# GFNet mixing with a SiLU MLP: another layout for one spill in DRAM, and another order for the conversion of the weights in the first twelve steps

## The chip, the core and the metric

The kernel runs on one core of a Trainium2 chip. The core has a matrix engine (TensorE, "PE" in the profile, with its weight loads listed apart as "PEld"), a vector engine (VectorE, "DVE"), a scalar engine (ScalarE, "ACT"), GpSimd ("POOL") and SyncE ("SP", which here only issues DMAs). Every engine works through its own queue in order, and waits where an instruction needs a result of another engine or of a DMA. The metric is the time of one execution on the device in microseconds (us).

## The reference

Eight sequences of 3008 rows with 256 channels each go through a filter in the frequency domain, and the result through a two-layer network with SiLU:

```python
X = np.fft.rfft(x, axis=1)
F = (filt_r + 1j * filt_i)[None, :, :]
y = np.fft.irfft(X * F, n=x.shape[1], axis=1)       # 8 x 3008 x 256
x = y.reshape(8 * 3008, 256)
h = x @ w_in                                        # 256 x 2048
out = (h * (1.0 / (1.0 + np.exp(-h)))) @ w_out      # 2048 x 256
```

The weights of the network arrive in 64-bit floats, the rest is used in 32-bit.

## The kernel before, in words

**Two halves.** The filter ("spectral part" of a batch entry `b`, the function `spectral`) is a DFT in stages with intermediate results in two DRAM tiles, `d1` and `d2`. The network takes tokens in pairs of blocks (`pairs`: 48 blocks of 2 x 256 or 2 x 240 tokens), and for each pair goes through the 2048 hidden channels in 8 steps of 256 (`jp` = 0 to 7). There are 384 steps. In step `s` TensorE alternates between a product of `hidden(s)` (the first layer) and one of `project(s - 1)` (the second layer), in 8 rounds. Pieces of the next batch entry's spectral part are put into these rounds: `put(step, round, piece, ...)` adds a piece to a list, and the loop at the end of the kernel emits, after every round, the pieces that are due. The order of every engine's queue is thus written out by hand; no scheduler moves anything.

**The opening.** Before step 0 stands the spectral part of `b = 0`: stage 1 (`stage1_first`), stage 2 (`forward`, `multiply`, `add`, `inverse_first`) for six groups `g`, and stage 3. `rows_first(g)` copies a group's two results out of PSUM (tiles `q`; for g = 5 a place in the weights' tile `w_t`) and calls `store_half(g, i, 0, queue)`, which stores the first half of the rows to `d2`: twelve stores. `fetch_rows` (line 745) reads them back in three calls of two DMAs on SP, for groups 0 and 1, 2 and 3, 4 and 5, into `us["t4"]`, from which `stage3(g)` computes for g = 0 to 3 (products `pd`, copied to `y` at line 783). The second halves are stored later (`halves_of`) and read by `load_t4` for groups 4 to 7 of stage 3. Beside this the opening holds stage 1 of `b = 1` (`stage1_pair`, three of them, their results `pa` copied by `out_pair` at line 447 and stored to `d1` by POOL in `store_rows`, line 467: 24 DMAs).

**The weights.** Sixteen blocks `j` of 512 KB of 64-bit words are loaded (`weights(j)`, line 1231, always on SP) and turned into 32-bit floats in pieces: `bits(j)` takes exponent and mantissa apart (two VectorE operations, lines 1249 and 1251), `added(j)` adds the low word (one, line 1265), `converted(j)` makes the exponent's scale (two ScalarE operations, lines 1258 and 1259), `signed(j)` puts the sign in (one VectorE operation, line 1270) and `placed(j)` multiplies and writes into `w_t` (one, line 1277). Blocks 2 jp and 2 jp + 1 make the group `jp`: one has the slots A11 and A12, the other S3 (which holds A21 at first) and A22. `combine_weights(jp, part)` makes the four sums that Strassen's scheme needs: part 0 writes S1, S2 and S4 (three operations), part 1 overwrites S3 (one); without a part both.

**Plain and Strassen steps.** The first six steps (`hidden_plain`, PARTS) do without the sums: pair 0 with jp 0, 1 and pair 1 with jp 0 to 3. Then come pair 0 with jp 2 to 7 (steps 6 to 11) and pair 1 with jp 4 to 7 (steps 12 to 15), by Strassen's scheme with seven products a step instead of eight and with sums by VectorE between them: the first product's copy `abc` (ScalarE, line 1034) and the second one's PSUM bank `pyz` give `g` (VectorE, line 997 called at 1037); the fourth product goes into the same bank `pyz`, and so waits until that sum has read it. `tokens(pair)` makes the sums of the tokens that these steps need (three VectorE operations). From step 16 on all pairs run in Strassen's scheme.

**Sums that are spilled.** Where a pair's accumulators (`acc`, four banks `i` = 0 to 3) are emptied, `drain` (line 1130) copies them to a tile `s`: banks 1 and 3 by VectorE, 0 and 2 by ScalarE. For pairs 0 and 1 this happens twice, since their steps are split: the first time (not `final`) after step 1 and after step 5, and later sums are added to what was spilled.

Of the kernel before, what the change touches and what calls it, by code (L numbers as in the profile page):

```python
# [274 lines left out]
def kernel(  # L275
# [96 lines left out]
    def spectral(b):  # L372
# [3 lines left out]
        d2 = dpool.tile([2 * NS, 32, 2, C] if b else [2, 2, 2 * NS, 16, C], FP32, name=f"d2_{b}", tag="d2")  # L376
# [325 lines left out]
        def rows_first(g):  # L702
# [11 lines left out]
            for i, qt in enumerate(tiles):  # L714
                last = g == NG - 1
                (nc.vector.tensor_copy if last and i else nc.scalar.copy)(out=qt, in_=halves[g][i])
                store_half(g, i, 0, nc.gpsimd if g == 4 or g == 5 and i else nc.sync if i else nc.scalar)

        def store_half(g, i, half, queue):

            a0 = 8 * g + 4 * i
            queue.dma_start(out=d2[half, :, a0:a0 + 4].rearrange("h a n c -> (a n) h c"), in_=us["q", g][i][half::2])
# [17 lines left out]
        def load_t4(g):  # L740
            t4s[g] = t4pool.tile([128, 4, C], FP32, name=f"t4_{b}_{g}", tag="t4")
            for h in range(2):
                nc.sync.dma_start(out=t4s[g][64 * h:64 * h + 2 * NS], in_=d2[1, h, :, 4 * g - 16:4 * g - 12, :])

        def fetch_rows(a0, n, *queues):

            k, r0 = divmod(a0, 16)
            for h in range(2):
                queues[h].dma_start(out=us["t4"][64 * h:64 * h + 64].rearrange("(q r) n c -> q r n c", r=4)[r0:r0 + n, k],
                                in_=d2[0, h, a0:a0 + n])  # L750
# [379 lines left out]
    def drain(pair, i, hs, final):  # L1130
# [5 lines left out]
        copy = v.tensor_copy if i % 2 else nc.scalar.copy  # L1136
# [117 lines left out]
    def convert_weights(*js):  # L1254

        for j in js:
            e, ef = raws[j][2], raws[j][4]
            nc.scalar.activation(out=ef, in_=e, func=AFT.Relu, scale=-1.0, bias=bias_t[:, 0:1])
            nc.scalar.activation(out=e, in_=ef, func=AFT.Relu, scale=-float(1 << 23), bias=bias_t[:, 1:2])
# [45 lines left out]
    def converted(*js):  # L1305
        if wide:
            convert_weights(*js)

# [93 lines left out]
    weights(2)  # L1402
# [20 lines left out]
    bits(2)  # L1423
# [9 lines left out]
    weights(3, 4, 5)  # L1433
# [41 lines left out]
    for step, rnd, *todo in (  # L1475
            (0, 2, (converted, 3)), (0, 3, (signed, 3), (placed, 3), (weights, 7, 8, 9, 10)), (0, 4, (bits, 4), (added, 4)),
            (0, 6, (bits, 5), (added, 5)), (1, 0, (converted, 4)), (1, 2, (converted, 5), (signed, 4), (placed, 4)),
            (1, 3, (signed, 5), (placed, 5)), (1, 5, (bits, 6), (added, 6)), (1, 6, (combine_weights, 2, 0)),
            (2, 0, (bits, 7), (added, 7)), (2, 1, (converted, 6)), (2, 3, (signed, 6), (placed, 6), (weights, 11)),
            (2, 4, (converted, 7)), (2, 5, (bits, 8), (added, 8)), (2, 6, (signed, 7), (placed, 7), (weights, 12)),  # L1480
            (2, 7, (combine_weights, 3, 0)), (3, 0, (bits, 9), (added, 9)), (3, 1, (converted, 8)),
            (3, 3, (signed, 8), (placed, 8), (weights, 13)), (3, 4, (converted, 9)), (3, 5, (bits, 10), (added, 10)),
            (3, 6, (signed, 9), (placed, 9), (weights, 14)), (3, 7, (combine_weights, 4)), (4, 0, (bits, 11), (added, 11)),
            (4, 1, (converted, 10)), (4, 3, (signed, 10), (placed, 10), (weights, 15)), (4, 4, (converted, 11)),
            (4, 5, (bits, 12), (added, 12)), (4, 6, (signed, 11), (placed, 11)), (4, 7, (combine_weights, 5)),
            (5, 0, (bits, 13), (added, 13)), (5, 1, (converted, 12)), (5, 2, (combine_weights, 2, 1)),
# [86 lines left out]
```

## Time and profile before

| | |
|---|---|
| median of 3 runs | 2502.34 us |
| the runs | 2502.74, 2496.92, 2502.34 us |
| the profiled execution: its own time | 2500.59 us |
| its span, first to last instruction | 2498.7 us |
| mean granted TensorE clock in it | 0.998 |

In a row of the timeline stand the start in us from the span's start, the length, the engine, the line, the operation, the tile written and the tiles read, the shape, the count, and in brackets how long the engine was idle before it and what ended that. A 32-bit matmul of 256 columns stands as two instructions. "SPq" and "ACTq" are the queues' own instructions, such as the issue of a DMA. In the list of waits stand the engine and line that waited, what it waited for, the total, the number of times and the longest. In the table of stretches stand busy time and number of instructions of each engine, the granted clock, the mean busy share of the 16 DMA engines and GB/s. A DMA queue's row has packets, MB and the share of 16 engines' time.

### The profile page before, as it was taken

How to read it: one execution, taken by the hardware profiler on the slowest of the kernel's cores; microseconds unless marked ns; L12 is line 12 of the kernel's file. 1: busy time of each engine (PE TensorE's matmuls, PEld its weight loads, DVE VectorE, ACT ScalarE, POOL GpSimd, SP SyncE). 2: the span in 40 equal slices, each digit the busy share in tenths (PEclk: the TensorE clock that was granted, in tenths of full speed). 3: DMA queues.
4: the chain of work that ended last, by engine and by line, in shares of the span. 5: the costliest groups of instructions: out<-in, count | busy, mean ns of one | idle time of the engine just before them, and what ended most of it. 6: DMA issues, size and time to landing. Idle time of an engine off the chain costs nothing.

```text
span 2498.7 us, 42324 instructions
## 1 busy us (share of the span) xinstructions
PE 2481.6 (99%) x16272; PEld 2128.3 (85%) x16272; DVE 1751.1 (70%) x3582; ACT 1087.2 (44%) x2984; POOL 442.6 (18%) x690
## 2 busy tenths in 40 slices
PE   9999999999999999999999999999999999999999
PEld 6778888888888888888888888888888888888988
DVE  7776677777777777777777867777677767655544
ACT  3534444444444444444444444444444444444443
POOL 4221112112121122211122112211221111101100
PEclk9999999999999999999999999999999999999999
DMA  8423233213242032420333103321142211200000
GB/s 311 146 86 100 66 72 85 76 30 81 60 98 72 21 93 54 114 62 22 80 80 95 55 26 91 79 68 43 35 107 53 56 44 34 63 21 9 17 9 17
DMA packets 137657, 170.68 MB, mean 68 GB/s; under 512 B 21052, under 2 KB 111644, under 8 KB 136828
## 3 DMA queue, kind: packets, MB, share of 16 engines
q1 hardware_dynamic: 113648, 121.01, 18.3%
q0 software_dynamic: 22800, 46.07, 7.1%
q8 instruction: 128, 2.10, 0.3%
q10 hardware_dynamic: 1008, 0.90, 0.1%
q14 instruction: 73, 0.60, 0.1%
HBM read 96.06 MB, written 81.26 MB: 71 GB/s over the span
## 4 chain that ended last, share of the span: by engine, by line
PE 97%; DVE 2%; DMA 0%; ACT 0%; issue 0%; POOL 0%; DVEq 0%; SPq 0%
PE acc L1118 45%; PE px L1026 25%; PE pyz L1026 19%; PE pd L801 1%; PE pf L524 1%; PE pc L620 1%; PE pb L582 1%; PE pc L698 0%; DVE g L997 0%; PE pa L404 0%; PE pd L764 0%; PE pb L564 0%; DVE w_t L997 0%; PE pc L678 0%; DVE w_t L1277 0%; DMA d<-w_t 0%
## 5 line engine op out<-in xcount | busy, mean ns | idle before, releaser
L1118 PE MATMUL acc<-g,w_t 128*128 128x256 f32 (+1 forms) x5388 | 1512.9, 376 | 3.1 <-ACT o L814 2.5
L1118 PEld LDWEIGHTS acc<-g,w_t 128*128 128x128 f32 x5388 | 1019.3, 190 | 154.8 <-ACT o L814 15.3
L997 DVE TENSOR_TENSOR g<-pyz,abc 128x256 f32<-128x256 f32 (+1 forms) x1134 | 471.5, 416 | 478.3 <-ACT abc L1047 236.2
L997 DVE TENSOR_TENSOR g<-g 128x512 f32<-128x512 f32 (+1 forms) x1134 | 581.2, 513 | 193.6 <-ACT g L1030 180.7
L1026 PE MATMUL px<-ty,w_t 128*128 128x256 f32 (+1 forms) x2268 | 665.2, 375 | 0.0
L1030 ACT ACTIVATE g<-g 128x256 f32<-128x256 f32 (+1 forms) x1134 | 465.3, 410 | 237.4 <-DVE g L997 237.4
L997 POOL TENSOR_TENSOR s<-s 128x256 f32<-128x256 f32 (+1 forms) x331 | 254.1, 785 | 1407.7 <-DVE s L1146 967.6
L1026 PEld LDWEIGHTS px<-ty,w_t 128*128 128x128 f32 x2268 | 427.9, 190 | 53.3 <-issue 1.8
L1026 PE MATMUL pyz<-y,w_t 128*128 128x256 f32 (+1 forms) x1512 | 444.0, 375 | 1.6 <-DVE g L997 1.4
L1026 PEld LDWEIGHTS pyz<-y,w_t 128*128 128x128 f32 x1512 | 278.8, 189 | 44.4 <-DVE g L997 5.0
L1041 ACT COPY abc<-px 128x256 f32<-128x256 f32 (+1 forms) x378 | 139.0, 368 | 368.6 <-PE px L1026 368.6
L1047 ACT COPY abc<-px 128x256 f32<-128x256 f32 (+1 forms) x378 | 139.2, 368 | 308.7 <-PE px L1026 308.6
L1030 ACT ACTIVATE g<-px 128x256 f32<-128x256 f32 (+1 forms) x378 | 143.6, 380 | 298.4 <-PE px L1026 298.4
L1026 PE MATMUL pyz<-ty,w_t 128*128 128x256 f32 (+1 forms) x756 | 222.4, 376 | 3.0 <-DVE g L997 2.9
L1026 PE MATMUL px<-y,w_t 128*128 128x256 f32 (+1 forms) x756 | 223.4, 377 | 1.1 <-ACT g L1030 0.5
L1026 PEld LDWEIGHTS px<-y,w_t 128*128 128x128 f32 x756 | 141.4, 189 | 22.9 <-DVE q L822 1.9
L1026 PEld LDWEIGHTS pyz<-ty,w_t 128*128 128x128 f32 x756 | 139.7, 190 | 24.0 <-DVE g L997 4.0
L1034 ACT COPY abc<-px 128x256 f32<-128x256 f32 (+1 forms) x378 | 133.0, 352 | 34.2 <-PE px L1026 34.2
L544 POOL DMA_DIRECT2D d<-tf x96 | 48.5, 505 | 212.8 <-DVE tf L474 212.7
L1146 ACT COPY s<-acc 128x512 f32<-128x512 f32 (+2 forms) x96 | 54.5, 568 | 49.3 <-issue 28.5
L641 POOL DMA_DIRECT2D d<-low x36 | 22.3, 618 | 292.4 <-DVE low L637 254.2
L514 DVE TENSOR_TENSOR uf<-x_all 120x512 f32<-120x512 f32 (+1 forms) x72 | 60.2, 863 | 0.6 <-DMA xr<-in_x_dram 0.3
(135 smaller groups left out, 1407.2 us busy)
## 6 DMA issues: line engine op xcount, KB each, us to landing
t<-d SPq DMA_DIRECT2D x84, 256.0 KB
t<-d SPq DMA_DIRECT2D x224, 96.0 KB
out_dram<-s SPq DMA_DIRECT2D x64, 256.0 KB
d<-q POOLq DMA_DIRECT2D x48, 256.0 KB, 5.3
x_all<-in_x_dram SPq DMA_DIRECT2D x96, 96.0 KB
x_all<-xr SPq DMA_DIRECT2D x96, 96.0 KB
d<-tf POOLq DMA_DIRECT2D x96, 96.0 KB, 2.7
d<-tq POOLq DMA_DIRECT2D x96, 96.0 KB, 2.8
```

The lines of the kernel that those rows point to most:

```text
L514: nc.vector.tensor_tensor(out=out, in0=in0, in1=in1, op=op)
L524: nc.tensor.matmul(out=ps[q][32 * k:32 * k + 32], lhsT=wq_t[rows, k], rhs=rhs[k][rows], start=True, stop=True)
L544: nc.gpsimd.dma_start(out=d1[par, :, grp, at:at + 4], in_=part[rows].rearrange("p q n c -> p (q n) c"))
L582: nc.tensor.matmul(out=ps[k, ri][32 * j:32 * j + 32, a, :], lhsT=dn_t[rows, 4 * (g + a) + at, :], rhs=t2s[g + a][rows, at, :], start=True, ...
L997: eng.tensor_tensor(out=out, in0=in0, in1=in1, op=op)
L1026: nc.tensor.matmul(out=out, lhsT=w_t[:, jp, c, 0], rhs=rhs, start=start, stop=True, skip_group_check=True)
L1030: nc.scalar.activation(out=g[:, k, 0:n], in_=g[:, k, 0:n] if src is None else src, func=AFT.Silu)
L1034: nc.scalar.copy(out=sums[:, 0, 0:n], in_=xo)
L1041: nc.scalar.copy(out=sums[:, 1, 0:n], in_=xo)
L1047: nc.scalar.copy(out=sums[:, 2, 0:n], in_=xo)
L1118: nc.tensor.matmul(out=acc[pair][i][:, h, 0:n], lhsT=w_t[:, jp, OUT_PLACE.get(c, c), 1], rhs=g[:, k, 0:n], start=i not in touched, stop=la ...
L1146: copy(out=dst, in_=src)
```

## The change

1. `d2` of `b = 0` gets another order of its axes. A row store now writes runs of 2 KB instead of 1 KB, and the fetches (`fetch_rows`, `load_t4`) read runs of 1 KB instead of 16 KB and 4 KB.
2. The last of the twelve stores, (g, i) = (5, 1), goes out on SP instead of POOL. In SP's queue it stands between the first fetch (which is issued before group 4 and 5 are done) and the second.
3. The load of block 3 moves from behind the fetches to the place right behind block 2's; its bits and its conversion move into the opening, ahead of stage 3, its signing and placing between stage 3's copies. POOL makes the sums S1, S2, S4 of group 0 in the opening.
4. Two copies of stage 1's last results change engines, one goes behind stage 3's first copy; the bank counter is set back by one after the idle matmuls, so that stage 3 takes other PSUM banks.
5. The table of pieces for steps 0 to 14 is written anew. The two ScalarE operations of a block's conversion are put two rounds apart (`converted_part`). Blocks 13 to 15 are rounded in steps 6 to 10, groups 6 and 7 combined in steps 8 and 10. Group 0's last sum and group 1's sums move from steps 13 and 14 to steps 5, 10 and 11; `tokens(0)` moves by two rounds.
6. Sums that are spilled for the first time are all copied by ScalarE.

```diff
-        d2 = dpool.tile([2 * NS, 32, 2, C] if b else [2, 2, 2 * NS, 16, C], FP32, name=f"d2_{b}", tag="d2")
+        d2 = dpool.tile([2 * NS, 32, 2, C] if b else [2, 2 * NS, 16, 2, C], FP32, name=f"d2_{b}", tag="d2")
...
-                store_half(g, i, 0, nc.gpsimd if g == 4 or g == 5 and i else nc.sync if i else nc.scalar)
+                store_half(g, i, 0, nc.gpsimd if g == 4 else nc.sync if i else nc.scalar)
...
-            queue.dma_start(out=d2[half, :, a0:a0 + 4].rearrange("h a n c -> (a n) h c"), in_=us["q", g][i][half::2])
+            queue.dma_start(out=d2[half, a0:a0 + 4].rearrange("a n h c -> (a n) h c"), in_=us["q", g][i][half::2])
...
-                nc.sync.dma_start(out=t4s[g][64 * h:64 * h + 2 * NS], in_=d2[1, h, :, 4 * g - 16:4 * g - 12, :])
+                nc.sync.dma_start(out=t4s[g][64 * h:64 * h + 2 * NS], in_=d2[1, :, 4 * g - 16:4 * g - 12, h, :])
...
-                                in_=d2[0, h, a0:a0 + n])
+                                in_=d2[0, a0:a0 + n, :, h, :])
...
-        copy = v.tensor_copy if i % 2 else nc.scalar.copy
+        copy = v.tensor_copy if i % 2 and final else nc.scalar.copy
...
+    def converted_part(part, j):
+        if wide:
+            convert_weights(j, part=part)
...
-    weights(2)
+    weights(2, 3)
...
-    bits(2)
+    bits(2, 3)
...
-    weights(3, 4, 5)
+    weights(4, 5)
...
     placed(0, 1)
+    combine_weights(0, 0, gp)
+    added(3)
...
-    converted(2)
-    out_of(2, 0, 1, 2, copy=act)
-    out_of(2, 3, copy=dve)
+    converted(2, 3)
+    out_of(2, 0, 1, copy=dve)
+    out_of(2, 2, copy=act)
...
     halves_of(2, 3)
+    weights(6)
+    idle(4, m=96)
+    early[0] -= 1
+    part["stage3"](0)
+    out_of(2, 3, copy=act)
+    part["stage3"](1)
+    signed(2)
+    placed(2)
+    part["stage3"](2)
+    signed(3)
+    placed(3)
     for u in (4, 5, 0, 1, 2, 3):
         second["store_rows"](u)
     halves_of(4, 5, 0, 1)
-    weights(6)
-    idle(4, m=96)
-    for g in range(3):
-        part["stage3"](g)
-    bits(3)
-    added(3)
-    signed(2)
-    placed(2)
...
-            (0, 2, (converted, 3)), (0, 3, (signed, 3), (placed, 3), (weights, 7, 8, 9, 10)), (0, 4, (bits, 4), (added, 4)),
...
-            (5, 0, (bits, 13), (added, 13)), (5, 1, (converted, 12)), (5, 2, (combine_weights, 2, 1)),
-            (5, 3, (signed, 12), (placed, 12)), (5, 4, (converted, 13)), (5, 5, (bits, 14), (added, 14)),
-            (5, 6, (signed, 13), (placed, 13)), (5, 7, (combine_weights, 6)), (6, 0, (converted, 14)),
-            (6, 1, (signed, 14), (placed, 14)), (6, 5, (bits, 15)), (7, 1, (combine_weights, 3, 1), (added, 15)),
-            (7, 2, (converted, 15)), (8, 1, (signed, 15), (placed, 15)), (9, 1, (combine_weights, 7)),
-            (13, 1, (combine_weights, 0)), (14, 1, (combine_weights, 1))):
+            (0, 7, (weights, 7, 8, 9, 10), (bits, 4), (added, 4)), (1, 1, (bits, 5), (added, 5)),
+            (1, 1, (converted_part, 0, 4)), (1, 3, (converted_part, 1, 4)), (1, 4, (signed, 4), (placed, 4)),
...
+            (4, 3, (signed, 10), (placed, 10), (weights, 15)), (4, 5, (converted_part, 0, 11)),
+            (4, 7, (converted_part, 1, 11)), (4, 5, (bits, 12), (added, 12)),
+            (4, 7, (signed, 11), (placed, 11)), (5, 1, (converted_part, 0, 12)),
+            (5, 3, (converted_part, 1, 12)), (5, 0, (combine_weights, 5)),
+            (5, 3, (signed, 12), (placed, 12)), (5, 5, (combine_weights, 2, 1)),
+            (5, 6, (combine_weights, 1, 0)), (6, 1, (combine_weights, 3, 1), (bits, 13), (added, 13)),
+            (6, 5, (bits, 14)), (7, 0, (converted, 13)), (7, 1, (signed, 13), (placed, 13), (added, 14)),
+            (7, 5, (bits, 15)), (8, 0, (converted, 14)), (8, 1, (combine_weights, 6)), (8, 5, (added, 15)),
+            (9, 0, (converted, 15)), (9, 1, (signed, 14), (placed, 14), (signed, 15)), (9, 5, (placed, 15)),
+            (10, 1, (combine_weights, 7)), (10, 5, (combine_weights, 0, 1)),
+            (11, 5, (combine_weights, 1, 1))):
...
-        step, rnd = combines[pair % per] if pair > 2 else ((5, 0), (11, 1), (12, 1))[pair]
+        step, rnd = combines[pair % per] if pair > 2 else ((5, 2), (11, 1), (12, 1))[pair]
```

The function `convert_weights(j, part)` does its first ScalarE operation unless `part` is 1, its second unless `part` is 0. In each block's turn in steps 1 to 4 the new table keeps the order bits, added, signed, placed and takes a block every half step.

More of the change, by code (lines that the diff above doesn't have):

```diff
@@ L1480 @@
[L1480 to L1484, printed above, removed]
@@ new lines @@
+            (2, 1, (converted_part, 0, 6)), (2, 3, (converted_part, 1, 6)), (2, 1, (bits, 7), (added, 7)),
+            (2, 3, (signed, 6), (placed, 6), (weights, 11)), (2, 5, (converted_part, 0, 7)),
+            (2, 7, (converted_part, 1, 7)), (2, 4, (bits, 8), (added, 8)), (2, 7, (signed, 7), (placed, 7)),
+            (3, 0, (combine_weights, 3, 0)), (3, 1, (converted_part, 0, 8)), (3, 3, (converted_part, 1, 8)),
+            (3, 1, (bits, 9), (added, 9)), (3, 3, (signed, 8), (placed, 8), (weights, 12, 13)),
@@ new lines @@
+            (3, 5, (converted_part, 0, 9)), (3, 7, (converted_part, 1, 9)), (3, 5, (bits, 10), (added, 10)),
+            (3, 7, (signed, 9), (placed, 9), (weights, 14)), (4, 1, (converted_part, 0, 10)),
+            (4, 3, (converted_part, 1, 10)), (4, 0, (combine_weights, 4)), (4, 2, (bits, 11), (added, 11)),
+            (4, 3, (signed, 10), (placed, 10), (weights, 15)), (4, 5, (converted_part, 0, 11)),
+            (4, 7, (converted_part, 1, 11)), (4, 5, (bits, 12), (added, 12)),
+            (4, 7, (signed, 11), (placed, 11)), (5, 1, (converted_part, 0, 12)),
```

14 lines of the change are left out of this document (7 added, 7 removed).

## The prediction

> **What bounds the kernel now.** I read the page first (busy times, then the chain that ended last), then the busy times by stretch, the list of what TensorE waited for, and the timeline around each of those waits.
>
> ```profile
> PE 2481.6 (99%) x16272; PEld 2128.3 (85%) x16272; DVE 1751.1 (70%) x3582; ACT 1087.2 (44%) x2984; POOL 442.6 (18%) x690
> ...
> PE 97%; DVE 2%; DMA 0%; ACT 0%; issue 0%; POOL 0%; DVEq 0%; SPq 0%
> ```
>
> TensorE (PE) is the bound: it is busy 99% of the span and makes 97% of the chain. The edits touch nothing after step 14, and the order of the matmuls stays as it is, so a gain can only be TensorE's waiting in the first 170 us. By stretch (columns: stretch, length, busy time of PE, PEld, DVE, ACT, POOL, granted clock, DMA share, GB/s):
>
> ```profile
> core 0: us, PE busy (x) PEld busy (x) DVE busy (x) ACT busy (x) POOL busy (x), PEclk, DMA share, GB/s
> 60.00:80.00 20.00, 20.00 (x152) 17.43 (x151) 18.12 (x36) 12.49 (x25) 13.67 (x25) 1.00 0.86 283
> 80.00:100.00 20.00, 17.49 (x80) 14.74 (x78) 19.21 (x40) 10.70 (x21) 0.00 (x0) 1.00 0.41 129
> 400.00:2450.00 2050.00, 2047.40 (x12912) 1768.67 (x12911) 1441.35 (x2943) 898.05 (x2498) 346.21 (x528) 1.00 0.23 58
> ```
>
> From 400 to 2450 us there are 2.6 us to win in 2050, and no edit reaches there. In 60 to 100 us VectorE (DVE) is busy 37.3 of 40 us: it converts the weights there, and can make TensorE wait. What TensorE waited for in the whole run (total, times, longest):
>
> ```profile
> PE pyz L1026 <- DVE g L997: 4.3, 4, 2.9
> ...
> PE pb L564 <- DVE p L657: 1.3, 1, 1.3
> ...
> PE px L1026 <- ACT g L1075: 0.5, 1, 0.5
> ...
> PE pyz L1072 <- ACT g L1075: 0.4, 1, 0.4
> ```
>
> The longest one is in step 6, the first that needs VectorE between its products:
>
> ```profile
> 96.99 0.59 PE L1026 MATMUL px<-ty,w_t 128*128 128x256 f32 x2
> 97.42 0.59 PE L1118 MATMUL acc<-g,w_t 128*128 128x256 f32 x2
> 100.87 1.05 PE L1026 MATMUL pyz<-ty,w_t 128*128 128x256 f32 x2 [2.86 <-DVE g L997]
> ...
> 104.82 0.59 PE L1026 MATMUL px<-ty,w_t 128*128 128x256 f32 x2
> ```
> ```profile
> 95.97 0.42 DVE L1249 TENSOR_SCALAR e<-raw 128x512 uint32<-128x512 uint32 x1
> ...
> 96.76 0.69 DVE L1265 SCALAR_TENSOR_TENSOR m<-raw,m 128x512 f32<-128x512 uint32 x1
> 97.37 0.68 DVE L1270 SCALAR_TENSOR_TENSOR e<-raw,e 128x512 uint32<-128x512 uint32 x1
> 98.08 0.69 DVE L1277 SCALAR_TENSOR_TENSOR w_t<-m,e 128x512 f32<-128x512 f32 x1
> 98.81 1.68 DVE L997 TENSOR_TENSOR w_t<-w_t 128x256 f32<-128x256 f32 x4
> 100.41 0.41 DVE L997 TENSOR_TENSOR g<-pyz,abc 128x256 f32<-128x256 f32 x1
> ```
>
> The first sum g could have started at about 97; it starts at 100.41, behind bits, rounding and combining for weights that no matmul needs before step 10. From start to start these rows also price VectorE's pieces, when it is never idle: the two bits 0.79 and added 0.61, 1.40 us a weight, signed and placed 0.71 + 0.73 = 1.44, a combination of four 1.60, of three about 1.2.
>
> **The clock.** A long wait costs twice:
>
> ```profile
> 46.50:49.90 3.40, 2.23 (x20) 1.14 (x12) 1.22 (x2) 2.11 (x4) 0.00 (x0) 1.00 0.87 233
> 49.90:53.30 3.40, 3.33 (x125) 3.36 (x128) 0.55 (x1) 0.48 (x1) 3.02 (x6) 0.50 0.96 316
> 94.20:97.60 3.40, 2.88 (x14) 2.22 (x13) 3.33 (x8) 2.70 (x6) 0.00 (x0) 1.00 0.00 0
> 97.70:101.10 3.40, 0.54 (x3) 0.23 (x2) 3.26 (x8) 0.70 (x3) 0.00 (x0) 1.00 0.00 0
> 101.10:104.50 3.40, 3.40 (x9) 2.69 (x9) 2.13 (x4) 0.54 (x2) 0.00 (x0) 0.50 0.46 116
> ```
>
> After a stretch of 3.4 us in which PE was busy 0.54 or 2.23 us, the granted clock is 0.50 for the next 3.4; after 2.88 us it stays 1.00. From 100.87 to 104.82 ten matmul instructions take 3.95 us; at 0.215 each (a pair every 0.43 us, 96.99 to 97.42) they take 2.15. So the half clock cost 1.8 us there. In 49.90 to 53.30, 125 small stage-3 matmuls took 3.33 us, 26.6 ns each; warm, 64 of them take 1.18, 18.4 ns (row at 63.05 below): 125 × 8.2 = 1.0 us. The Trainium skill's "TensorE: Matmul & The Clock Gate" (Part 1: The HAM clock gate) has the half clock come after at least one idle window of about 3.4 us. By that rule neither gap here, both with some work in the window, would have cost clock, and the sum below would be 2.8 us smaller, 2493.8; the trace disagrees, with 0.50 behind 0.54 and 2.23 busy of 3.40.
>
> **Part 1: opening, DMA.** Stage 3 waits for the third fetch of d2, and that for the last store:
>
> ```profile
> SPq L749 <- DMA d<-w_t: 4.1, 1, 4.1
> ...
> 45.71 1.10 SPq L749 DMA_DIRECT2D w_t<-d  x2
> ```
> ```profile
> 38.34 1.48 POOL L722 DMA_DIRECT2D d<-q  x2 [2.50 <-ACT q L716]
> 40.21 0.76 POOL L722 DMA_DIRECT2D d<-w_t  x1 [0.40 <-DVE w_t L716]
> ...
> DMA to landing us min/median/max: 4.4/5.4/7.3
> ...
> 49.97 4.53 PE L764 MATMUL pd<-wi_t,w_t 64*64 64x47 f32 x190 [0.76 <-DMA w_t<-d]
> ```
>
> SP stands 4.1 us for the store that POOL issued at 40.21; that landed 5.4 us later and the third fetch went out at 45.71. The store moves to SP, right when VectorE's copy is done, near 39.95. Its landing from SP is not shown; bounds are the 4.4 and 7.3 us of POOL's stores at line 722. Nothing can go before POOL's other stores, the second begun near 39.1: 43.5 to 44.5. I take 44.6 for the third fetch, a gain of 1.1. Against it: the store is queued on SP behind the first fetch and ahead of the second, and the 512 KB of weight 3 now pass at 29.6 ahead of a row store and of x's third pair. The pieces:
>
> ```profile
> q1 hardware_dynamic: 129, 0.79, 87.2%
> ...
> q1 hardware_dynamic: 1088, 1.05, 70.7%
> ```
>
> The first row is 46.5 to 49.9 us (pieces of 16 and 4 KB): 0.872 × 16 × 3.4 us for 0.79 MB, 60 ns per KB; the second 125 to 131 us (1 KB pieces, the form of the new fetches): 66 ns. A fetch of 256 KB gives each of 16 engines 16 KB, so 0.1 us more each, 0.2 for the last two. Stores of 2 KB instead of 1 KB I take as nothing. Net: PE starts 0.9 us earlier (bounds: 2 earlier, 1 later). Then the window that held 2.23 us of work holds about 3.1, above the 2.88 that kept its clock: 1.0 us more. Weight 3's bits and conversion fill idle time ahead of stage 3 (from 46.50 to 49.90 VectorE is busy 1.22 and ACT 2.11 of 3.40 us); POOL's three combinations end before the fetch lands.
>
> **Part 2: steps 0 to 5.**
>
> ```profile
> 58.64 0.59 PE L1072 MATMUL px<-y,w_t 128*128 128x256 f32 x2
> ...
> 63.05 1.18 PE L764 MATMUL pd<-wi_t,w_t 64*64 64x47 f32 x64
> ...
> L1146 ACT COPY s<-acc 128x512 f32<-128x512 f32 (+2 forms) x96 | 54.5, 568 | 49.3 <-issue 28.5
> ```
>
> A pair of matmul rows lasts 0.59 and starts every 0.43, so each wait costs the idle shown plus 0.16. In step 0 ACT had a conversion between two silus; it has none now: 0.4 + 0.16, say 0.5. At the entry to step 6 (the 0.5 of the list) the conversion of weight 13 stood ahead of a silu; it is gone from there: 0.7. ACT gets the four spilled sums (0.57 or less each), but the conversion is cut in two halves of 0.72, one between two silus; a silu may be 1.3 us late before PE waits, and 0.72 + 0.57 just fits. I cost it at nothing; without that cover, some 0.3 a time.
>
> VectorE in steps 1 to 5: the copy of y after stage 3's fourth group now stands ahead of weight 4's rounding, so VectorE waits for it, until 5.6 us into step 1 (63.05 + 1.18 − 58.64). From there it runs without a pause: nine signed and placed (weights 4 to 12) 13.0, seven bits and added (6 to 12) 9.8, combinations (2,0) and (3,0) 2.4, 4 and 5 3.2, the tokens' three sums 1.5, (2,1) and (1,0) 1.6, and 0.7 where ACT's halves come late: 32.2 us behind the copy's 0.5, so the first sum can start at 38.3. PE takes 8.2 us for step 1 (with stage 3) and 6.9 for each of four more: step 6 begins at 35.8, and its fourth product is due at 38.4 (35.8 + 3 × 0.86), with the sum done, 0.4 after its start. So the wait of 2.86 + 0.16 shrinks to about 0.3, and with it goes the half clock: 3.0 + 1.8 − 0.3 = 4.5 us. What left this stretch: bits, adding and rounding of 13, bits and adding of 14, combination 6 (1.40 + 1.44 + 1.40 + 1.60) and 1.1 us of copies; (1,0) came in.
>
> **Part 3: steps 6 to 14.** A step is 6 us of PE; its sums take VectorE 2.8. What is added per step (bits, adding, rounding of 13 to 15, combinations 6 and 7, single differences) is at most 2.9, and 2.2 between two sums, behind sums that are not due for 2 us: nothing on the path. In step 13 the 4 combining operations of weights 0, ahead of the products, go:
>
> ```profile
> 154.85 2.27 DVE L997 TENSOR_TENSOR w_t<-w_t 128x256 f32<-128x256 f32 x3
> ...
> 166.36 0.70 PE L1026 MATMUL pyz<-y,w_t 128*128 128x256 f32 x2 [0.32 <-DVE g L997]
> ```
>
> They take over 2.27 us and PE waits 1.3 behind them (the wait of pb on p in the list): 1.45 saved. Step 14 loses combination 1 the same way: 0.48.
>
> **The sum**: 0.9 + 1.0 + 0.5 + 0.7 + 4.5 + 1.45 + 0.5 = 9.6 us off the profiled execution's 2500.59: **2491.0**. That execution lies 1.75 under the median of the runs.
>
> **The rivals.** (a) VectorE stays late: its chain has no slack, and beside POOL's work three combining operations took 2.27 us instead of 1.26. If it slips 2.5 us, the wait of step 6 returns with its half clock: 2491.0 + 4.3 = 2495.3. For it: the sum would start at 38.3 and should be done at 38.4. Against: in those steps POOL computes nothing, it only issues DMAs. (b) The opening gains nothing: the new store waits behind the fetch in one queue, lands no earlier, stage 3 starts cold, maybe 1 us later: 2491.0 + 1.9 + 1 = 2493.9. For it: a DMA share of 0.87 already. (c) Slower: ACT's first spilled copy goes into the tile that held x's third pair and must wait for eight of POOL's row stores:
>
> ```profile
> L467 POOL DMA_DIRECT2D d<-t x24: 498/501/691, 52.9 to 72.2; - x24
> ...
> DMA to landing us min/median/max: 2.3/5.3/7.9
> ```
>
> The eighth goes out near 60 and lands by 68; the copy is due at 68 (step 2 from 66.8 − 2.4, and four products on). On VectorE that wait held nothing; on ACT it holds every silu. A landing x us late costs x − 1.5, with the half clock 1.8 more; from x = 9.3 on the kernel is slower than before: at x = 12, 2491.0 + 12.3 = 2503.3. Against: it needs twice the longest landing.
>
> **How the numbers follow.** Forecast 0.65, with a range of its own of 2487 to 2495; (a) 0.17, (b) 0.12, (c) 0.06. 0.3% of this kernel is 7.5 us, about what a measurement can tell: faster than that means under 2493.1 by the profiled execution's time. Of the forecast 0.58 lies there, of (a) and (b) 0.08; 0.27 of all lies within, and 0.07 slower, (c) and the unforeseen. The range: the bounds of part 1 (−1, +3) and of part 2 (+4.3), and the 6 us between the runs of one kernel: 2486 to 2498.
>
> **What would show it.** Right: PE's wait for g in step 6 under 1 us and granted clock 1.00 from 90 to 110 us; no wait of pb in step 13; stage 3 starting near 49.1 and step 0 near 52.5. Wrong: a wait of px or pyz on ACT in steps 2 to 5, a wait of ACT's copy on DMA, SP standing longer than 2 us for the last store, or a new wait of steps 7 to 11 on VectorE.

## The result

The changed kernel takes 2491.39 us (median of 6 runs, 2490.58 to 2494.34), the kernel before 2501.18 us beside it (6 runs, 2496.92 to 2502.92): a ratio of 0.9964, 95% interval 0.9951 to 0.9977. The forecast was 2491.0. The execution profiled after is the slowest of the six: 2494.34 us, span 2491.8.

The page of the changed kernel, busy times and the chain that ended last:

```profile
PE 2479.1 (99%) x16272; PEld 2126.5 (85%) x16272; DVE 1747.9 (70%) x3576; ACT 1087.5 (44%) x2987; POOL 443.6 (18%) x692
...
PE 98%; DVE 1%; DMA 0%; ACT 0%; issue 0%; POOL 0%; SPq 0%; DVEq 0%
```

TensorE bounds it as before. Stretches of the changed kernel, with the columns of the prediction's table:

```profile
52.00:55.40 3.40, 2.29 (x119) 2.06 (x120) 1.27 (x3) 1.28 (x4) 1.98 (x5) 1.00 1.02 357
60.00:80.00 20.00, 20.00 (x153) 17.42 (x152) 15.47 (x31) 12.17 (x25) 13.66 (x26) 1.00 0.83 267
80.00:100.00 20.00, 20.00 (x94) 17.45 (x93) 19.24 (x41) 9.94 (x22) 0.00 (x0) 1.00 0.50 161
400.00:2450.00 2050.00, 2047.49 (x12914) 1768.91 (x12913) 1441.24 (x2941) 898.66 (x2500) 347.81 (x527) 1.00 0.23 58
```

In 80 to 100 us TensorE is now busy all 20.00 (17.49 before), and VectorE no less than before: 19.24. 400 to 2450 is as it was. What TensorE waited for in the changed kernel (total, times, longest):

```profile
PE acc L1118 <- ACT o L814: 2.5, 3, 0.8
PE pc L698 <- issue: 1.6, 1, 1.6
PE pyz L1026 <- DVE g L997: 1.1, 2, 0.6
...
PE px L1026 <- ACT g L1030: 0.5, 1, 0.5
```

Gone are the 2.9 us wait of pyz, the 1.3 of pb, and both on g of L1075. New, and not in the prediction, is 1.6 us of pc on "issue". Step 6, TensorE and then VectorE:

```profile
98.27 0.59 PE L1118 MATMUL acc<-g,w_t 128*128 128x256 f32 x2
98.70 0.68 PE L1026 MATMUL pyz<-ty,w_t 128*128 128x256 f32 x2
```
```profile
96.62 1.67 DVE L997 TENSOR_TENSOR w_t<-w_t 128x256 f32<-128x256 f32 x4
98.21 0.42 DVE L997 TENSOR_TENSOR g<-pyz,abc 128x256 f32<-128x256 f32 x1
```

In before the sum g started at 100.41 and the product that needs it at 100.87. Now the sum starts at 98.21, right behind the four combining operations, and the product goes out at 98.70, on its beat of 0.43, without a wait. The opening of the changed kernel, TensorE and then SP's queue:

```profile
38.99 0.66 PE L698 MATMUL pc<-w_t,minus 64*64 64x256 f32 x8 [1.59 <-issue]
...
53.70 3.09 PE L764 MATMUL pd<-wi_t,w_t 64*64 64x47 f32 x190 [0.95 <-DMA w_t<-d]
```
```profile
43.92 0.49 SPq L722 DMA_DIRECT2D d<-w_t  x1
44.58 5.32 SPq L749 DMA_DIRECT2D w_t<-d  x4
```

Stage 3 (190 matmuls) takes 3.09 us instead of 4.53: no half clock. But it starts at 53.70, not at 49.97. From the chain that ended last (start, length, what), before and then changed: the last store up to its landing, the issue of the third fetch on SP, its second DMA up to its landing.

```profile
40.21 5.37 DMA d<-w_t
45.71 0.47 SPq L749
46.22 3.66 DMA w_t<-d
```
```profile
43.92 4.41 DMA d<-w_t
48.41 0.51 SPq L749
48.96 4.49 DMA w_t<-d
```

VectorE's last copy, whose result the last store writes, ends at 39.91 us in before and at 43.90 in the changed kernel. So the fetch goes out 4.51 us behind it instead of 5.80, but lands 5.05 us after that (53.46) instead of 4.17 (49.88).

**One account for both kernels.** The order of the 16272 matmuls is the same in both, so each can be compared with itself: its start in the changed kernel minus its start in before. That difference changes only where time is lost or won. "Again" is a second profile of the changed kernel (below); us, minus is a gain.

```
                                        forecast  first profile  again
first full clock of the opening             -          +2.67      +0.11
gap ahead of matmul 472 (pc on issue)       -          +1.50      +0.95
start of stage 3 behind it                -0.9         -0.44      -0.61
stage 3 itself (half clock)               -1.0         -1.44      -1.44
step 0                                    -0.5         -0.65      -0.65
entry to step 6                           -0.7         -0.79      -0.79
step 6, wait and half clock               -4.5         -4.73      -4.73
step 13                                   -1.45        -1.89      -1.89
step 14                                   -0.5         -0.59      -0.58
elsewhere                                   -          -0.23      -0.29
sum                                       -9.6         -6.59      -9.92
```

The first row is not the change's: the half-clocked start of the opening lasts differently long in each execution (last section). Its rows of stage 1, before and changed, are the same 96 matmuls:

```profile
6.03 10.85 PE L404 MATMUL pa<-w_t,wx 32*128 32x512 f32 x96
```
```profile
6.45 13.11 PE L404 MATMUL pa<-w_t,wx 32*128 32x512 f32 x96
```

The trace's records of the granted clock begin with the first full clock, at 5.51 us in before and at 11.03 in this profile; for the time ahead of the first record the table of stretches prints 1.00, and the matmuls' pace shows that it was not full. Without the first row the change is worth 9.3 and 10.0 us.

### The profile page after: what moved, and what is told of

Its sections match the earlier page's. It is cut to its first block, busy times and chain, and to the rows that moved or that the text cites. A ratio compares the mean times of both kernels' runs of the same rounds, so it can differ in the third digit from the quotient of the medians.

```text
span 2491.8 us, 42324 instructions
## 1 busy us (share of the span) xinstructions
PE 2479.1 (99%) x16272; PEld 2126.5 (85%) x16272; DVE 1747.9 (70%) x3576; ACT 1087.5 (44%) x2987; POOL 443.6 (18%) x692
## 3 DMA queue, kind: packets, MB, share of 16 engines
q1 hardware_dynamic: 116064, 121.15, 18.4%
## 4 chain that ended last, share of the span: by engine, by line
PE 98%; DVE 1%; DMA 0%; ACT 0%; issue 0%; POOL 0%; SPq 0%; DVEq 0%
PE acc L1118 46%; PE px L1026 26%; PE pyz L1026 19%; PE pd L801 1%; PE pf L524 1%; PE pc L620 1%; PE pb L582 1%; PE pa L404 1%; PE pc L698 0%; PE px L1072 0%; PE pyz L1072 0%; PE pb L564 0%; PE pd L764 0%; PE pc L678 0%; PE idle L1353 0%; DVE g L997 0%
```

## The experiments

Each of the twelve kernels is the changed one with the edit shown, but for e6. Where a delay of stage 3 is given, it is counted from the end of VectorE's last copy of the inverse transform (10.06 us in before, 9.80 in the changed kernel).

**e1: the rounding back ahead of step 6.**

```
-            (5, 3, (converted_part, 1, 12)), (5, 0, (combine_weights, 5)),
+            (5, 3, (converted_part, 1, 12)), (5, 0, (bits, 13), (added, 13), (combine_weights, 5)), (5, 4, (converted, 13)),
+            (5, 5, (bits, 14), (added, 14)), (5, 6, (signed, 13), (placed, 13)),
...
-            (5, 6, (combine_weights, 1, 0)), (6, 1, (combine_weights, 3, 1), (bits, 13), (added, 13)),
-            (6, 5, (bits, 14)), (7, 0, (converted, 13)), (7, 1, (signed, 13), (placed, 13), (added, 14)),
+            (5, 6, (combine_weights, 1, 0)), (6, 1, (combine_weights, 3, 1)),
```

> The changed kernel with VectorE's work on weights 13 and 14 back before step 6: bits, adding, rounding of 13 and bits and adding of 14 (1.40 + 1.44 + 1.40 = 4.24 us by the rows of before), and the whole conversion of 13 back between silus; combination 6 stays late. Theory A (the wait of step 6 is the length of VectorE's queue, and VectorE has no idle time left before it; its first sum started at 98.21, PE took its product at 98.70 without a wait): PE waits 4.2 us for g in step 6, the window behind is granted half clock (1.8 more), about 2497.5. Rival B (the gain of step 6 came from the spilled copies' move and the shorter conversions; the rounding fits in idle time): wait under 1 us, time as the changed kernel's 2491.4. Where the wait is under 1.5 us, no half clock by A either.

2497.83 us (median of 10), ratio to before 0.9985 (0.9975 to 0.9994). TensorE's timeline of this kernel and its stretches:

```profile
100.31 0.70 PE L1026 MATMUL pyz<-ty,w_t 128*128 128x256 f32 x2 [3.83 <-DVE g L997]
```
```profile
94.15:97.56 3.41, 2.33 (x11) 1.71 (x9) 3.34 (x8) 0.74 (x2) 0.00 (x0) 1.00 0.00 0
97.56:100.97 3.41, 0.67 (x3) 0.61 (x4) 2.92 (x7) 0.42 (x1) 0.00 (x0) 1.00 0.00 0
100.97:104.39 3.42, 3.42 (x10) 2.71 (x9) 0.42 (x1) 0.99 (x3) 0.00 (x0) 0.50 0.00 0
```

4.24 us of VectorE's work put back gave 3.83 us of wait, and a half-clocked stretch behind it. By matmul numbers step 6 costs 5.70 us more than in the changed kernel (4.2 and 1.8 expected). Theory A holds. VectorE's queue had next to no slack: counted from step 1's start the sum starts 4.01 us later than in the changed kernel and the product 4.00 (the idle 3.83, and the 0.16 by which pairs overlap). The work put back simply took 0.2 less than the 4.24.

This run says something of the entry to step 6, too. It has the whole conversion of weight 13 back where before had it, and no wait there (0.00 by matmul numbers). In before the conversion held a silu because it stood 2.19 us waiting for VectorE's bits:

```profile
93.36 0.72 ACT L1258 ACTIVATE e<-e,bias_t 128x512 f32<-128x512 uint32 x1 [2.19 <-DVE e L1249]
```

**e2: odd spilled sums on VectorE.**

```
-        copy = v.tensor_copy if i % 2 and final else nc.scalar.copy
+        copy = v.tensor_copy if i % 2 else nc.scalar.copy
```

> The changed kernel with the odd spilled sums copied by VectorE again: 2 of the 4 such copies that stand ahead of step 6's first sum, 0.55 each. Theory A (VectorE's queue has no slack): the first sum comes 1.1 later, PE waits about 0.9 to 1.1 us in step 6, and the granted clock stays 1.00 because the window still has over 2.3 us of work: +1.1, 2492.5. Rival B (the move of the copies is what made step 6 free): wait 2 us or more and half clock, 2495 or later. Rival C: the copies on ScalarE cost a silu somewhere and going back gains: 2491 or less, with no wait.

2493.37 us (median of 5), ratio 0.9966 (0.9953 to 0.9979). TensorE in step 6:

```profile
97.61 0.70 PE L1026 MATMUL pyz<-ty,w_t 128*128 128x256 f32 x2 [0.34 <-DVE g L997]
```

0.34 us, and 0.52 by matmul numbers: less than theory A's 0.9 to 1.1. From start to start the two copies take VectorE 0.61 and 0.34 us, 0.95 together instead of 1.1, and 0.4 of that falls into an idle 0.4 us that VectorE has ahead of 76.62 in the changed kernel (it waits there for ScalarE's conversion) and not here. B and C fall: the copies are a small part of the gain.

**e3: combinations of pairs 0 and 1 back in steps 13 and 14.**

```
-    combine_weights(0, 0, gp)
...
-            (5, 6, (combine_weights, 1, 0)), (6, 1, (combine_weights, 3, 1), (bits, 13), (added, 13)),
+            (6, 1, (combine_weights, 3, 1), (bits, 13), (added, 13)),
...
-            (10, 1, (combine_weights, 7)), (10, 5, (combine_weights, 0, 1)),
-            (11, 5, (combine_weights, 1, 1))):
+            (10, 1, (combine_weights, 7)), (13, 1, (combine_weights, 0)),
+            (14, 1, (combine_weights, 1))):
```

> The changed kernel with the combinations of weight pairs 0 and 1 whole on VectorE in steps 13 and 14 again, as before, and without the three operations of pair 0 that POOL does in the opening. Theory A: TensorE waits again 1.3 us in step 13 (pb on p) and 0.3 in step 14, as before: the matmuls behind step 14 start 2.0 + 0.5 us later against those ahead of step 13 than in the changed kernel; 2493.9. Rival B (those waits went because everything ahead came earlier, or because of the late rounding's other places): under 0.5 us.

2495.36 us (median of 7), ratio 0.9974 (0.9963 to 0.9985). VectorE, then TensorE:

```profile
150.05 2.61 DVE L997 TENSOR_TENSOR w_t<-w_t 128x256 f32<-128x256 f32 x4
152.57 0.68 DVE L657 TENSOR_TENSOR z<-pb,filt 128x512 f32<-128x512 f32 x1
153.17 0.68 DVE L657 TENSOR_TENSOR p<-pb,filt 128x512 f32<-128x512 f32 x1
```
```profile
153.91 1.09 PE L564 MATMUL pb<-t,d_t 64*32 64x256 f32 x30 [1.29 <-DVE p L657]
...
161.56 0.70 PE L1026 MATMUL pyz<-y,w_t 128*128 128x256 f32 x2 [0.32 <-DVE g L997]
```

The four combining operations stand ahead of the products again, and the same two waits are back, to the hundredth. The first of them in before:

```profile
158.71 1.09 PE L564 MATMUL pb<-t,d_t 64*32 64x256 f32 x30 [1.29 <-DVE p L657]
```

By matmul numbers all 2.48 us of the two steps are given back. A holds.

**e4: layout and queue of the opening back.** The store, and the layout at its four places:

```
-        d2 = dpool.tile([2 * NS, 32, 2, C] if b else [2, 2 * NS, 16, 2, C], FP32, name=f"d2_{b}", tag="d2")
+        d2 = dpool.tile([2 * NS, 32, 2, C] if b else [2, 2, 2 * NS, 16, C], FP32, name=f"d2_{b}", tag="d2")
...
-                store_half(g, i, 0, nc.gpsimd if g == 4 else nc.sync if i else nc.scalar)
+                store_half(g, i, 0, nc.gpsimd if g == 4 or g == 5 and i else nc.sync if i else nc.scalar)
```

> The changed kernel with the old layout of d2 (row stores of 1 KB, fetches of 16 KB) and the last store on POOL's queue again, ahead of nothing; weight 3's early load, POOL's combinations and the rest stay. Theory A (as the prediction had it): stage 3 starts 0.9 us later after VectorE's last copy than in the changed kernel (9.80 us from the copy's end to stage 3's first product there, 10.05 before), and the window ahead loses its clock: +1.9, 2493.3. Rival B (the traces of the two kernels: only 0.25 of start gained; third fetch goes out 1.2 earlier but takes longer): 0.3 later, clock half or not by the window's grid, 2491.7 or 2493.0. Rival C (the big gain in the opening is weight 3's early load): no later at all.

2494.8 us (median of 9), ratio 0.9973 (0.9963 to 0.9982). Stage 3 in this kernel:

```profile
54.76 4.58 PE L764 MATMUL pd<-wi_t,w_t 64*64 64x47 f32 x190 [0.87 <-DMA w_t<-d]
```

It starts 10.89 us after the copy, 1.1 later than in the changed kernel, and at half clock (4.58 against 3.09): 2.6 us by matmul numbers. A holds, and costs somewhat more than it had (1.9); B and C fall. One half-clocked stretch of 3.41 us takes 0.0007 off an execution's mean granted clock. Of this kernel's nine executions six have 0.999 and three 1.000, while all eleven of the changed kernel have 1.000 (six of the result, five in e10): the reversed edits bring the half clock back, but not every time.

**e5: weight 3's load later.** It moves behind nine more statements of the opening (the expectation says five).

```
-    weights(2, 3)
+    weights(2)
...
     inverse(2)
+    weights(3)
     products(5)
```

> The changed kernel with one line moved: weight 3's load (512 KB) is issued on SP's queue five statements later, behind x's third pair and the next row stores, where the engines of the DMA are half idle. Theory A: the new gap of TensorE in the inverse transform (0.8 to 1.9 us in the profiles of the changed kernel and of its variants, none in before, always ahead of matmul 472) is TensorE waiting for its own program: its third instruction packet of 16 KB was served 7.9 us after the second in before and 9.8 in the changed kernel, and weight 3's 32 KB on each DMA engine at 60 ns per KB are 1.9 us. With the load moved the packet comes 7.9 us behind the second again, the gap is under 0.3 and everything behind comes 1.3 to 1.6 earlier: 2489.9. Rival B (the gap has another cause: a semaphore that the profile doesn't show, or the places of VectorE's work): gap and time stay, 2491.4. Rival C: the load now delays the fetches of d2, and stage 3 starts as late as before in spite of the gap gone: 2491.4 without the gap.

2491.91 us (median of 6), ratio 0.9964 (0.9952 to 0.9977). TensorE around matmul 472, the first of the second row:

```profile
34.53 1.04 PE L698 MATMUL pc<-w_t,e_t 64*64 64x256 f32 x16
35.40 1.04 PE L698 MATMUL pc<-w_t,minus 64*64 64x256 f32 x16
```

No gap. The page of the changed kernel lists TensorE's program among the DMA queues (128 packets of 2.10 MB are 16 KB each), and in the trace's records of its packets the third can be followed:

```profile
q8 instruction: 128, 2.10, 0.4%
```
```
                          third packet's start      gap ahead of
                          behind the second's       matmul 472
before                          7.87                   0
e5                              7.95                   0
e11                             8.17                   0.10
e6                              9.00                   0.91
e8, e2, e10                     9.01  9.08  9.09       0.95  0.94  1.23
e3, e12, e7                     9.57  9.67  9.79       1.49  1.76  1.73
changed, e1, e9                 9.80  9.86  9.86       1.76  1.76  2.04
e4                             10.26                   2.03
```

Where the packet comes later than 8.2 us behind the second, the gap grows with it, us for us, and in all fourteen profiles matmul 472 starts 1.2 to 1.5 us after the packet ends. So the gap is, by all that these profiles show, TensorE without a program, which they can only call "issue". The three shortest delays are of kernels that load weight 3 late; all ten profiles with the early load have the gap. e6 loads it late and has 0.91: the early load is a cause, not the only one.

What stays open is the time. In the profiles 1.5 of the gap's 1.76 us count: between matmuls 60 and 500 this kernel loses 1.5 us less than the first profile of the changed one, since TensorE makes up 0.3 right behind the gap. But its median lies between the two of the changed kernel (2491.39, and 2492.59 in e10), while the half-clocked start moves single runs by up to 2.6 us. Five or six runs can't show the gain.

**e6: before, with layout and queue alone.**

```
-        d2 = dpool.tile([2 * NS, 32, 2, C] if b else [2, 2, 2 * NS, 16, C], FP32, name=f"d2_{b}", tag="d2")
+        d2 = dpool.tile([2 * NS, 32, 2, C] if b else [2, 2 * NS, 16, 2, C], FP32, name=f"d2_{b}", tag="d2")
...
-                store_half(g, i, 0, nc.gpsimd if g == 4 or g == 5 and i else nc.sync if i else nc.scalar)
+                store_half(g, i, 0, nc.gpsimd if g == 4 else nc.sync if i else nc.scalar)
```

> The kernel before with only the layout of d2 (row stores of 2 KB, fetches of 1 KB) and the last store on SP's queue ahead of the second fetch; weight 3's load and all of VectorE's and ScalarE's work as before. Theory A (these two edits gain about 1.2 us of start, as the reversed experiment gave, and the half clock of stage 3 with it, 1.35): stage 3 starts 8.8 us after VectorE's last copy (10.05 before), step 6 still waits 2.9 with its half clock: 2499. Rival B (they gain only in company of weight 3's early load): 10.05 again, 2501. No gap of TensorE ahead of matmul 472 by the theory of the instruction packet, since weight 3 comes late.

2499.76 us (median of 10), ratio 0.9991 (0.9982 to 1.0001). Its list of waits:

```profile
PE pyz L1026 <- DVE g L997: 4.3, 4, 2.9
...
PE pd L764 <- DMA w_t<-d: 1.5, 1, 1.5
PE pb L564 <- DVE p L657: 1.3, 1, 1.3
...
PE pc L698 <- issue: 0.7, 1, 0.7
```

All waits of before are there, and stage 3 starts 10.16 us after the copy: nothing gained in the start. The third fetch went out at 4.45 (5.80 in before), but took 5.47 us to land (4.17). What this profile gains in stage 3 is its clock (1.45 by matmul numbers). Since stage 3 starts no earlier than in before, one profile can't show that the edits won it. Neither theory had it so, and with an interval up to 1.0001 the time shows no gain.

**e7: the last store on POOL's queue, layout kept.** The diff is e4's last pair of lines.

> The changed kernel with the last store on POOL's queue alone (2 KB layout kept). Theory A: the store's issue behind POOL's two others is what the edit saves; the third fetch goes out about 1.2 us later after VectorE's last copy (4.5 us in the changed kernel, 5.8 before), stage 3 starts 0.9 to 1.2 later than 9.80. Rival B (the second fetch, which no longer stands behind the store, drains earlier and makes up for it): within 0.4 of 9.80.

One run: 2497.26 us.

```profile
53.03 0.42 PE L764 MATMUL pd<-wi_t,w_t 64*64 64x47 f32 x2 [2.15 <-issue]
54.78 5.10 PE L764 MATMUL pd<-wi_t,w_t 64*64 64x47 f32 x190 [1.34 <-DMA w_t<-d]
```

The third fetch goes out 6.92 us after the copy, stage 3 starts at 12.31, 2.5 later than in the changed kernel, at half clock throughout. Twice what A had; B falls. The first row's "issue" is here the wait for the fetch's first half, which landed at 52.94.

**e8: conversions whole again.** In steps 1 to 5, as here:

```
-            (1, 1, (converted_part, 0, 4)), (1, 3, (converted_part, 1, 4)), (1, 4, (signed, 4), (placed, 4)),
+            (1, 1, (converted, 4)), (1, 4, (signed, 4), (placed, 4)),
```

> The changed kernel with the conversions of weights 4 to 12 whole again (1.44 us on ScalarE in one piece, at the place of the first half). Theory A (the prediction's cover: a silu may be 1.3 us late; 1.44, with a spilled copy 2.0): TensorE waits 0.1 to 0.3 at most conversions, nine of them, some 1 to 2.5 us in all in steps 1 to 5; 2493.3. Rival B (conversions stood whole in before without a wait in steps 1 to 4): no wait, 2491.4.

2492.83 us (median of 5), ratio 0.9965 (0.9952 to 0.9977). No wait of TensorE on ScalarE in steps 1 to 5; from stage 3 on the matmuls keep the changed kernel's times within 0.2 us. B holds: whole conversions are covered too.

**e9: layout back, store on SP.** The diff is e4's without the store's pair of lines.

> The changed kernel with only the layout of d2 as before (row stores of 1 KB, fetches of 16 KB); the last store stays on SP. Theory A (the 1 KB pieces of the fetch are what the prediction mis-sized: the third fetch took 4.8 to 5.5 us from its issue to its landing in the eight kernels with them so far and 4.2 and 4.4 in the two with 16 KB pieces): fetch out 4.4 to 4.6 us after VectorE's last copy, landed 4.3 later, stage 3 at 8.9 to 9.1 instead of 9.5 to 10.1. Rival B (it took longer because the second fetch, queued behind the store, still drains, whatever the pieces): 9.5 or later. Rival C (row stores of 1 KB land later): fetch out at 5 or later.

One run: 2492.36 us.

```profile
51.78 3.09 PE L764 MATMUL pd<-wi_t,w_t 64*64 64x47 f32 x190 [0.83 <-DMA w_t<-d]
```

Fetch out at 4.52, landed 5.01 later, stage 3 at 9.77: A falls, B holds in this run. But the pieces are not out of it. Where the second fetch had landed before the third went out or within 0.3 us of it, 16 KB pieces took 4.17 and 4.42 us (before, e4) and 1 KB pieces 4.90 and 5.15 (e12, e7); e11, with 0.9 us of the second fetch to go, took 4.13 with 16 KB. Where it still had 1.7 to 3.2 us to go, eight profiles with 1 KB pieces took 4.8 to 5.5 and this one with 16 KB 5.01. So small pieces alone and the second fetch alone each go with some 0.7 us more, and both together with hardly more than one of them; 16 KB pieces behind a second fetch far from done were seen once.

**e10: the changed kernel again.**

> The changed kernel itself, beside its variants on one chip. 2491.4 again. In its profile the gap ahead of matmul 472 between 0.8 and 2.0 us (theory of the instruction packet: third packet 9 to 9.9 us behind the second); stage 3 9.5 to 10.1 us after VectorE's last copy; the first full clock anywhere between 5 and 11 us, and with it up to 2.6 us of the profiled time.

2492.59 us (median of 5), ratio 0.9966 (0.9954 to 0.9979); the profiled run took 2491.09.

```profile
35.88 0.66 PE L698 MATMUL pc<-w_t,minus 64*64 64x256 f32 x8 [1.05 <-issue]
...
50.42 3.09 PE L764 MATMUL pd<-wi_t,w_t 64*64 64x47 f32 x190 [0.40 <-DMA w_t<-d]
```

The profile is as expected (the median is 1.2 us above): third packet at 9.09, gap 1.2, stage 3 at 9.63, first full clock at 5.73 us (11.03 in the first profile). This one started as fast as before's, so its column is the cleanest account of the change.

**e11: e5 and e9 together, as a candidate.**

> The changed kernel with the old layout of d2 and weight 3's load five statements later, as a candidate that beats both. Theory A (both terms of the opening are real and add up): no gap ahead of matmul 472 (1.3 to 1.8 less), stage 3 at 8.9 to 9.1 after the copy (0.7 less): 2.0 to 2.5 us under the changed kernel of the same call, 2489.2. Rival B (what the gap costs is made up later, since the time of the kernel with the late load alone was 2491.9): within 1 us of the changed kernel.

2492.8 us (median of 5), ratio 0.9963 (0.9950 to 0.9977): it beats the kernel before, not the changed one. The gap is gone, but stage 3 starts 10.98 us after the copy at half clock, because the last store took 6.5 us to land (4.4 in e5 and e9). ScalarE's store, issued 0.16 us ahead of it on the other queue, took 6.5 as well, so it is not SP's queue alone. Why 1 KB row stores and the late load together delay it wasn't tried further.

**e12: second fetch ahead of the last store.**

```
+    part["fetch_rows"](16, 16, nc.sync, nc.sync)
     inverse(5)
-    part["fetch_rows"](16, 16, nc.sync, nc.sync)
```

> The changed kernel with the second fetch issued by SP ahead of the last store instead of behind it. Theory A (the store's issue is what counts, and a fetch of two DMAs takes SP about 1.2 us): the store goes out 0.3 to 0.7 later, the third fetch too; stage 3 0.3 to 0.5 later than the changed kernel's 9.5 to 10.1. Rival B (the second fetch drains 1.2 earlier and leaves the engines free for the third): 9.0 to 9.4.

One run: 2497.03 us. SP's queue, then the stretches of this kernel:

```profile
40.67 2.59 SPq L749 DMA_DIRECT2D w_t<-d  x4
43.30 0.65 SPq L722 DMA_DIRECT2D d<-w_t  x1
49.08 1.17 SPq L749 DMA_DIRECT2D w_t<-d  x2
```
```profile
49.11:52.52 3.41, 1.75 (x18) 0.83 (x10) 2.27 (x4) 2.20 (x4) 1.91 (x3) 1.00 0.61 156
52.52:55.94 3.42, 2.13 (x67) 2.04 (x70) 0.00 (x0) 0.00 (x0) 1.49 (x4) 0.50 0.93 332
55.94:59.35 3.41, 3.41 (x137) 3.41 (x130) 1.91 (x4) 1.44 (x3) 2.89 (x6) 0.50 0.90 324
```

The store goes out 0.8 us later than in the changed kernel, but lands 5.65 us after its issue instead of 4.4, now that the fetch stands ahead of it in the queue. Stage 3 starts at 11.75, with 6.8 us of half clock. Both theories fall in size: in this one run the store's place ahead of the second fetch is worth 1.95 us of stage 3's start, and the clock.

## Why the prediction was right

- **What bounds the kernel.** Right: nothing changed in 400 to 2450 us, and every gain is a wait or a half clock of the first 170 us.
- **Step 6.** Right, by its own working: the first sum was put at 38.3 us after step 1's start, with TensorE's need at 38.4; it starts at 37.94 (98.21 − 60.27), needed at 38.43. 4.73 us against 4.5, and e1 shows the cause. Rival (a), VectorE late, didn't occur, but it was near: the sum ends at 98.63 and the product is due at 98.70, and 0.95 us of copies were enough for a wait in e2.
- **Entry to step 6, step 0, step 14.** Right within 0.15 us each. For the entry the reason was half of it: the conversion of weight 13 held a silu because VectorE's bits for it were late, and with bits in time (e1) it holds none. Step 0's reason wasn't tried in a run of its own.
- **Step 13.** Right in cause (e3); the size was 1.89, not 1.45.
- **The half clock of stage 3.** Right in kind, 1.44 instead of 1.0: the warm price of a stage-3 matmul is 16.2 ns in this block (3.09 / 190), not the 18.4 of the row used. But the reason given, a window of 3.1 us of work, was wrong: the window 52.00 to 55.40 held 2.29, hardly more than before's 2.23, and kept its clock. What made before's lose it stays open; that the edits of the opening have to do with it rests on e4's nine executions against the changed kernel's eleven.
- **Part 1, the opening: the step that failed.** "A gain of 1.1" for the third fetch's issue was right (1.29: 4.51 us after the copy instead of 5.80), and so was the store's move as its cause (e7: 6.92 with the store on POOL). "0.2 for the last two" was mis-sized: the fetch took 5.05 us instead of 4.17, 0.9 more. Its 1 KB pieces and the second fetch, now queued behind the store, each account for some 0.7 of that where they come alone (e9), so which of them it was here stays open. (The 60 ns per KB under that term counts 1000 bytes and the 66 counts 1024; alike they are 61.5 and 66.2, and the term would have been smaller still.) And that the 512 KB of weight 3 "now pass at 29.6 ahead of a row store and of x's third pair" had no price of its own: with them TensorE's program came late, 1.0 to 1.5 us in the two profiles. "PE starts 0.9 us earlier" so became 0.3 to 1.1 us later (gap and start together). The start of stage 3 near 49.1 can't be set against the profile's 53.70 directly, as 2.67 us of that are the clock of the opening; in e10, which starts like before's, it is 50.42, and step 0 starts at 53.44, not near 52.5. One of the signs of being wrong did come: SP stands 2.1 us for the last store ("over 2 us"), 2.2 in e10.
- **Rival (b)** was half right: no gain in the opening's start, but no cold stage 3. Its reason fails: from SP the store lands in 4.41 us, not 5.37.
- **Rival (c)** did not occur: ScalarE's spilled copies waited for no DMA. **ScalarE's cover**: right to cost at nothing; e8 shows that the halves weren't needed for it.
- **The sum.** 9.6 forecast, 9.92 in the profile that starts like before's, 9.8 between the medians. The opening came out 1.2 us worse than forecast (−0.9 became +0.34 in the second profile), and larger sizes in steps 6 and 13, in stage 3 and elsewhere made up for it: the total is better than its parts, and that these cancel is luck.

## What to carry to other kernels

Where an engine runs the same list of instructions in both kernels, compare each one's start with its own in the other trace: the difference steps exactly where time is won or lost, and it separates a change from what one execution does at its start. In an opening that waits for DMA, count what else is under way: here a load put earlier went with TensorE's own program coming 1 to 2 us late, and a store ahead of a fetch in one queue was worth more than the issue time it saves. A wait shown as "issue" has a cause too; look among the DMA's packets.

## What the runs showed of the hardware

**TensorE's program comes by DMA and can be late.** 16 KB packets, some 254 of its matmuls and weight loads to each (2 × 16272 / 128); where the third came 1.1 to 2.4 us later behind the second than in before, TensorE stood. The Trainium skill's "DMA: Bandwidth & Descriptors" (Queues, rings and completion order) has each DMA engine go round between the queue rows packet by packet; by that rule a bulk load should cost a program packet little. These runs show 0.9 to 2.0 us of gap with the load ahead and none with it behind in e5 (0.1 in e11, but 0.9 in e6), and no record names the engine that served the packet, so the mechanism stays open.

**The first full clock is a matter of the execution.** It came between 5.40 and 11.03 us in the fourteen profiles: 5.40, 5.51, 5.73 and 6.00 in four, 8.15 to 8.25 in three, 9.87 to 11.03 in seven. Each us of delay costs about half a us: 2.5 of the 3.25 us between the two profiled runs of the changed kernel (2494.34 and 2491.09) are this. The Trainium skill's "TensorE: Matmul & The Clock Gate" (Part 1: The HAM clock gate) calls the warm-up run-variable, with its window free-running; the traces agree, but with a spread of 5.6 us, more than one window of 3.4.

**How little work keeps the clock.** In all fourteen traces the granted clock's changes lie whole multiples of 3.413 us apart. In the stretches of that length between them, the half clock followed 0.55, 0.67, 1.35, 1.57, 1.69 and 1.75 us of busy TensorE (and went on after 1.65 and 2.13); the full clock stayed after 1.83, 1.86, 1.91, 1.93, 1.97, 2.12, 2.16, 2.20 and more. Only before's 46.47 to 49.88, with 2.26 (2.23 in the prediction's window), doesn't fit, and it is the one that stage 3's 1.44 us hang on. So partly idle stretches do cost the clock, as the prediction had it, and all the stretches at full clock but this one divide near 1.8 us, not near 2.5; busy time alone doesn't decide it. Nor does the kernel: of the 47 executions of before that ran beside the experiments, three have a mean granted clock of 1.000, room for no half-clocked stretch at all, and take 2496.6 to 2497.1 us.
